# A recurrent attention with a three-way max feed-forward: the first up projection folded into the down projection, the weights loaded at other places

## The chip, the cores and the metric

The kernel runs on one core of a Trainium2 chip. The metric is the time of one execution on the device in microseconds (us), and less is better. Beside the runs there is one profiled execution, and the length of its trace, from the first to the last instruction, is called its span.

## The reference

A gated linear recurrence (4 batches, 8 heads, 768 steps, 48 values a head) gives 3072 rows of 384 values. They go through a feed-forward layer of three up projections, their maximum, and one down projection.

```python
state = alpha[:, :, t, :, None] * state + np.einsum('bhd,bhe->bhde', k[:, :, t], v[:, :, t])
y[:, :, t] = np.einsum('bhd,bhde->bhe', q[:, :, t], state)
...
h = np.maximum(np.maximum(x @ w1, x @ w2), x @ w3)
return (h @ w_out).astype(np.float32)
```

`w1`, `w2` and `w3` are 384 x 768 and `w_out` is 768 x 384, all of them float32, 1152 KB each. q, k, v and alpha are 4.7 MB each, and the output is 4.7 MB.

## The kernel before

**Tiles.** The sequence is cut into 6 chunks of 128 steps. With 4 batches this makes 24 units `u`, one chunk of one batch with its 8 heads. Two units make a group `n`, so there are 12 groups. The attention of a unit runs through `prep(u)` and `output(u)`: the logarithm of alpha on ACT (`decay`, L370), a running sum on PE (L413), two exponentials on ACT (L416, L418), products with q and k (L425, on POOL or DVE as the table `EARLY` says, else on POOL), a cast of v (L436, POOL, or L431, ACT), 8 transposes on PE (L446) with a copy out on DVE (L450), 8 score matmuls (L458), a masked copy on DVE (L464), the output matmuls (L481, L484), a scaled copy on ACT (L492), 3 transposes (L499) and a copy on DVE into `xT` (L503). `state(u)` carries the state to the next chunk (L517, L523 on DVE, L530 on POOL).

**The feed-forward layer of a group, `ffn(n)`.** For each of 3 pairs of 128 hidden columns and each of the 3 up projections, PE runs 6 matmuls with 256 moving columns (L554). The first projection is copied out of PSUM by ACT (L562); each of the other two goes through a maximum on DVE (L566). For each of the two units of the group there are then 6 matmuls with 384 columns for the down projection (L579), a copy on ACT (L587) and a store (L590).

**Loads.** All loads of q, k, v and alpha and all stores are issued from the SP queue. Loads of a group go into one of 5 buffers per tensor. Group 0 is loaded in halves (one unit each), every other group whole, 384 KB a tensor. The four weights are issued from the POOL queue by `weights(g, gate)` (L359), which casts to float16 on the way. Each waits for the k product of a unit: `w1` for unit 2, `w2` and `w3` for unit 3, `w_out` for unit 5.

**The order of the work** is written out at build time. Every step gives its engine, an assumed cost, a rank and what it reads and writes (`plan.step`); `Plan.order` goes through the steps in assumed time, puts them in order on each engine, and gives each its PSUM banks (8 in all). `Transfers` is its model of the two DMA queues. On the chip each engine works through its list in that order and waits where the next step is not ready. The feed-forward steps of a group have a rank `LEAD` behind the attention steps of the same group.

Of the kernel before, what the change touches and what calls it, by code (L numbers as in the profile page):

```python
# [21 lines left out]
NBANKS = 8  # L22
# [1 line left out]
TURN_RANK, TURN_COST = 2.0, 0.1  # L24
SP_FIRST = 0.9
QUEUES = ("SP", "POOL")
DMA_IN, DMA_OUT, DMA_SLOW = 0.9, 0.9, 1.0
DMA_BOTH = {"SP": 0.3, "POOL": 0.7}


class Transfers:


    def __init__(self):
        self.now = 0.0
        self.jobs = {e: [] for e in QUEUES}

    def add(self, e, arrival, work, i):
        self.jobs[e].append([arrival, work * DMA_SLOW, i])

    def next(self, commit=False):
        now = self.now
        left = {e: [list(j) for j in js[:1]] for e, js in self.jobs.items()}
        while True:
            heads = [(e, js[0]) for e, js in left.items() if js]
            if not heads:
                return None
            on = [(e, j) for e, j in heads if j[0] <= now + 1e-9]
            later = [j[0] for _, j in heads if j[0] > now + 1e-9]
            if not on:  # L50
                now = min(later)
                continue
            rate = DMA_BOTH if len(on) > 1 else dict.fromkeys(QUEUES, 1.0)
            e, j = min(on, key=lambda x: x[1][1] / rate[x[0]])
            end = now + j[1] / rate[e]
            if later and min(later) < end:
                for f, k in on:
                    k[1] -= (min(later) - now) * rate[f]
                now = min(later)
                continue  # L60
            if commit:
                for f, k in on:
                    self.jobs[f][0][1] = k[1] - (end - now) * rate[f]
                for f, k in heads:
                    if (f, k) not in on:
                        self.jobs[f][0] = k
                self.jobs[e].pop(0)
                self.now = end
            return end, j[2]


class Plan:
# [55 lines left out]
    def order(self):  # L128
# [19 lines left out]
                pending[self.steps[i][0]].add(i)  # L148
        free = dict(dict.fromkeys(HOP, 0.0), SP=SP_FIRST)
        bank_free = {b: 0.0 for b in range(NBANKS)}  # L150
        place, seq, recent = {}, [], []
        dma, mode = Transfers(), 0

        def finish(i, done):
# [15 lines left out]
        while len(seq) < n:  # L170
# [12 lines left out]
                if pick is not None and (best is None or pick < best[0]):  # L183
                    best = (pick, e)
            landing = dma.next()
            if landing and (best is None or landing[0] + DMA_OUT <= best[0][0]):
                end, i = dma.next(commit=True)
                self.landed[i] = end + DMA_OUT
                finish(i, end + DMA_OUT)
                continue  # L190
            (t, _, i), e = best
            _, cost, _, _, _, banks, load, m = self.steps[i]
# [5 lines left out]
            if e == "PE":  # L198
                if m != mode:
                    mode = m  # L200
                    cost += TURN_COST
                recent = [(a, b) for a, b in recent if b > t - 4.0]
                if sum(b - max(a, t - 4.0) for a, b in recent) < 2.0:
                    cost *= 2
                recent.append((t, t + cost))
            free[e] = t + cost
            seq.append((t, i))
            if load:
                dma.add(e, t + cost + DMA_IN, load, i)
            else:  # L210
                finish(i, t + cost + HOP[e])
            if i in follows:
# [6 lines left out]
def kernel(  # L219
# [76 lines left out]
    Zs = [homes(B, [P, NP, 2 * D], FP16, f"Z{i}_") for i in range(2)]  # L296
    e12s = homes(4, [P, HG // 2, 2], FP32, "e")
    Gs = homes(3, [P, HG // 2], FP32, "G")
    wcat = sb.tile([P, NFT, 3, DF], FP16, name="wcat")
    wo16 = sb.tile([P, NJ, DM], FP16, name="wo16")  # L300
    zero = sb.tile([P, 2 * P], FP16, name="zero")
    nc.vector.memset(zero, 0.0)
    for t in las:
        nc.vector.memset(t[:, :, D:], 0.0)
    for t in qks:
# [2 lines left out]
        for t in zz:  # L308
            nc.vector.memset(t, 0.0)

    plan = Plan({x: range(NBANKS) for x in ("Lp", "hp", "tp", "A", "yp", "xp", "pp", "gp", "op", "fill")})
    place = {}

    psall = pspool.tile([P, NBANKS, 512], FP32, name="psum")
# [10 lines left out]
    def banks2(key, dtype):  # L325
# [1 line left out]
        return both if dtype == FP32 else both.bitcast(dtype)  # L327

    live = {}
    LEAD = 7.5  # L330
    WAFTER = {2: (0,), 3: (1, 2), 5: (3,)}
    FILL = 0
    EARLY = {0: ("DVE", "DVE", "POOL"), 1: ("POOL", "DVE", "POOL"),
             3: ("DVE", "POOL", "POOL"), 5: ("POOL", "DVE", "POOL"),
             6: ("DVE", "POOL", "POOL"), 7: ("DVE", "POOL", "ACT")}


    views = {n: x.rearrange("b h s d -> s (b h) d") for n, x in
# [14 lines left out]
                      load=1.8 * (hi - lo) / HG)  # L353

    def weights(g, gate):
        w, dst = ((moe_w1, moe_w2, moe_w3, moe_w_out)[g],
                  wo16 if g == 3 else wcat[:, :, g, :])
        plan.step("POOL", 0.78, -1.0,
                  lambda: nc.gpsimd.dma_start(dst, w.rearrange("(t p) f -> p t f", p=P)),  # L359
                  reads=[gate], writes=[("w", g)], line="weights", load=3.5)  # L360


    def decay(n):
# [8 lines left out]
                      reads=[("a", n % 5, h) for h in range(lo // H, hi // H)],  # L372
                      writes=[("la", n % 3, h) for h in range(lo // H, hi // H)])

        if n == 0:
            ln(0, H)
            ln(H, HG)
        else:
            ln(0, HG)
        key = ("hp", n)  # L380

        def totals():
# [156 lines left out]
    def ffn(n):  # L539
        cb, g0 = divmod(n, B // UB)  # L540
        xT, hT = xTs[n], hTs[n % 3]
        npieces = 3 * (NJ // 2) + UB
        rank = [2 * n + LEAD + 2.0 * i / npieces for i in range(npieces)]
        for j in range(NJ // 2):
            for g in range(3):
                r = rank[3 * j + g]
                gk = ("gp", n, j, g)

                def grow(j=j, g=g, gk=gk):
                    live[gk] = bank(gk, [P, 2, TG], FP32)  # L550
                    for jj in range(2):
                        c0 = (2 * j + jj) * P
                        for kt in range(NFT):
                            nc.tensor.matmul(live[gk][:, jj, :], wcat[:, kt, g, c0:c0 + P],  # L554
                                             xT[:, kt, :], start=(kt == 0), stop=(kt == NFT - 1))

                plan.step("PE", 0.656, r, grow, banks=[gk],
                          writes=[gk] + ([("room", n % 3, j)] if g == 0 else []),
                          reads=[("room", n % 3, j)] * (g > 0) + [("w", g), ("xT", n, 0), ("xT", n, 1)])
                h = hT[:, 2 * j:2 * j + 2, :]  # L560
                if g == 0:
                    plan.step("ACT", 0.59, r, lambda h=h, gk=gk: nc.scalar.copy(out=h, in_=live[gk]),  # L562
                              reads=[gk], writes=[("hT", n % 3, j)])
                else:
                    plan.step("DVE", 0.69, r,
                              lambda h=h, gk=gk: nc.vector.tensor_max(h, live[gk], h),  # L566
                              reads=[gk, ("hT", n % 3, j)], writes=[("hT", n % 3, j)])
        for i in range(UB):
            b = g0 * UB + i
            m = n * UB + i  # L570
            r = rank[3 * (NJ // 2) + i]
            ok = ("op", m)
            parts = [(0, NJ)] if n < NG - 1 else [(0, NJ - 2), (NJ - 2, NJ)]
            for lo, hi in parts:
                def shrink(i=i, ok=ok, lo=lo, hi=hi):
                    if lo == 0:
                        live[ok] = bank(ok, [P, DM], FP32)
                    for kt in range(lo, hi):
                        nc.tensor.matmul(live[ok], hT[:, kt, i * P:(i + 1) * P], wo16[:, kt, :],  # L579
                                         start=(kt == 0), stop=(kt == NJ - 1))  # L580

                plan.step("PE", 0.1627 * (hi - lo), r + (0.5 if lo else 0.0), shrink,
                          banks=[ok] if lo == 0 else [], writes=[ok, ("ob room", m % 4)],
                          reads=[(x, n % 3, j) for x in ("hT", "room")
                                 for j in range(lo // 2, hi // 2)]
                          + [("w", 3)])
            plan.step("ACT", 0.49, r, lambda m=m, ok=ok: nc.scalar.copy(out=obs[m % 4], in_=live[ok]),  # L587
                      reads=[ok], writes=[("ob", m % 4)])
            plan.step("SP", 0.4, -2.0,
# [2 lines left out]
                      reads=[("ob", m % 4), ("ob room", m % 4)], load=0.5)  # L592


    def fill(count):
        for i in range(count):
            def run(i=i):
                if i == 0:
                    live[("fill",)] = bank(("fill",), [P, 2 * P], FP32)
                nc.tensor.matmul(live[("fill",)], zero[:, :P], zero, start=True, stop=True)  # L600

            plan.step("PE", 0.11, 99.0, run, banks=[("fill",)] if i == 0 else [],
                      writes=[("fill",)] if i == 0 else [], reads=[("fill",)] if i else [])

    fill(FILL)
    load(0, 0, H, "aqk")
    load(0, H, HG, "a")
    load(0, 0, H, "v")
    load(0, H, HG, "qkv")
    for n in range(NG):  # L610
        if n:
            load(n, 0, HG)
        decay(n)
        for u in range(n * UB - B, (n + 1) * UB - B):
            if u >= 0:
                state(u)
        for u in range(n * UB, (n + 1) * UB):
            prep(u)
            if u in WAFTER:
                for g in WAFTER[u]:  # L620
                    weights(g, ("qk", u % 7, 1))
            output(u)
        if n >= 4:
            ffn(n - 4)
    for n in range(NG - 4, NG):
# [36 lines left out]
```

## Time and profile before

| | us |
|---|---|
| median of 3 runs | 167.75 |
| lowest and highest run | 165.92, 167.81 |
| span of the profiled execution | 164.9 |

| engine | busy us in the span | what most of it is |
|---|---|---|
| PE | 145.3 | up projections L554 81.7, down projection L579 26.2 |
| DVE | 118.5 | maxima L566 47.7, masked scores L464 28.8 |
| ACT | 77.4 | copies L562 21.1, exponentials L416 and L418 11.9 each |
| POOL | 72.5 | products with q and k L425 41.2, state L530 15.7, casts of v L436 13.3 |

In the table busy time is the union of an engine's instructions. Matmuls overlap in it: a row such as "x648, 278 ns" gives the length of one matmul from its start to its modelled end, while a new one starts about every 109 ns. What a stream of matmuls costs is therefore read from the chain of waits, which gives the time from the first start to the next piece, not from the mean of one.

### The profile page before, as it was taken

How to read it: one execution, taken by the hardware profiler on the slowest of the kernel's cores; microseconds unless marked ns; L12 is line 12 of the kernel's file. 1: busy time of each engine (PE TensorE's matmuls, PEld its weight loads, DVE VectorE, ACT ScalarE, POOL GpSimd, SP SyncE). 2: the span in 40 equal slices, each digit the busy share in tenths (PEclk: the TensorE clock that was granted, in tenths of full speed). 3: DMA queues.
4: the chain of work that ended last, by engine and by line, in shares of the span. 5: the costliest groups of instructions: out<-in, count | busy, mean ns of one | idle time of the engine just before them, and what ended most of it. 6: DMA issues, size and time to landing. Idle time of an engine off the chain costs nothing.

```text
span 164.9 us, 4286 instructions
## 1 busy us (share of the span) xinstructions
PE 145.3 (88%) x1720; PEld 117.6 (71%) x1720; DVE 118.5 (72%) x204; ACT 77.4 (47%) x159; POOL 72.5 (44%) x104
## 2 busy tenths in 40 slices
PE   0555857869999999999999999999999999999991
PEld 0332635648867888889877898876898787878770
DVE  7464590088998999998999989993679685526460
ACT  3527362500466866557445765473634414252312
POOL 0043970070042899799917888829408000000000
PEclk9999985799999999999999999999999999999998
DMA  6999999999999999999899999995300020211112
GB/s 126 219 223 218 212 184 198 212 194 192 204 227 177 224 189 218 170 222 234 197 233 200 231 186 228 195 287 191 104 0 4 17 82 8 88 41 58 48 48 95
DMA packets 104884, 26.32 MB, mean 160 GB/s; under 512 B 99745, under 2 KB 104865, under 8 KB 104865
## 3 DMA queue, kind: packets, MB, share of 16 engines
q1 hardware_dynamic: 102592, 23.60, 70.0%
q0 software_dynamic: 1984, 2.36, 8.5%
q8 instruction: 13, 0.21, 0.5%
q10 hardware_dynamic: 288, 0.10, 0.3%
q14 instruction: 7, 0.05, 0.1%
HBM read 23.69 MB, written 4.72 MB: 172 GB/s over the span
## 4 chain that ended last, share of the span: by engine, by line
PE 75%; SPq 10%; DMA 9%; DVE 3%; issue 1%; ACTq 0%; ACT 0%; DVEq 0%
PE psum L554 40%; PE psum L579 14%; SPq L347 10%; DMA kn<-in_k_dram 9%; PE psum L446 5%; PE psum L458 3%; PE psum L484 2%; PE psum L499 2%; PE psum L481 2%; PE psum L413 2%; PE psum L517 2%; PE psum L385 1%; DVE qk L425 1%; DVE LA L464 1%; DVE qkT L450 1%
## 5 line engine op out<-in xcount | busy, mean ns | idle before, releaser
L554 PE MATMUL psum<-xT,wcat 128*128 128x256 f16 x648 | 81.7, 278 | 1.7 <-DMA wcat<-in_moe_w_dram 1.5
L554 PEld LDWEIGHTS <-wcat 128*128 128x128 f16 x648 | 62.3, 100 | 11.6 <-DMA wcat<-in_moe_w_dram 1.7
L566 DVE TENSOR_TENSOR hT<-psum,hT 128x512 f16<-128x512 f32 x72 | 47.7, 684 | 15.3 <-PE psum L554 13.0
L464 DVE TENSOR_TENSOR LA<-psum,c 128x1024 f16<-128x1024 f32 x24 | 28.8, 1217 | 6.5 <-PE psum L458 6.3
L425 POOL TENSOR_TENSOR qk<-kn,en 128x384 f16<-128x384 f32 x21 | 21.3, 1020 | 21.5 <-ACT en L418 11.5
L562 ACT CAST hT<-psum 128x512 f16<-128x512 f32 x36 | 21.1, 587 | 20.3 <-PE psum L554 19.5
L579 PE MATMUL psum<-wo,hT 128*128 128x384 f16 x144 | 26.2, 326 | 0.0
L425 POOL TENSOR_TENSOR qk<-qn,ep 128x384 f16<-128x384 f32 x20 | 19.9, 998 | 8.7 <-ACT ep L416 4.0
L587 ACT COPY ob<-psum 128x384 f32<-128x384 f32 x24 | 11.4, 481 | 22.4 <-PE psum L579 19.0
L492 ACT ACTIVATE xb<-psum,c 128x384 f16<-128x384 f32 x24 | 13.9, 585 | 14.9 <-PE psum L484 14.9
L436 POOL TENSOR_SCALAR v<-vn,c 128x384 f16<-128x384 f32 x23 | 13.3, 586 | 15.6 <-DMA vn<-in_v_dram 11.9
L530 POOL TENSOR_TENSOR Z<-U,G 48x192 f16<-48x192 f32 x32 | 15.7, 503 | 9.6 <-DVE U L523 8.5
L450 DVE COPY qkT<-psum 128x1024 f16<-128x1024 f16 x24 | 16.3, 685 | 4.7 <-PE psum L446 4.5
L446 PE MATMUL psum<-c,qk 128*128 128x128 f16 x192 | 16.1, 234 | 3.4 <-DVE qk L425 3.4
L579 PEld LDWEIGHTS <-hT 128*128 128x128 f16 x144 | 13.5, 98 | 7.6 <-DVE hT L566 0.2
L416 ACT ACTIVATE ep<-psum 128x384 f32<-128x384 f32 x24 | 11.9, 497 | 12.6 <-PE psum L413 12.0
L446 PEld LDWEIGHTS <-qk 128*128 128x128 f16 x192 | 13.1, 105 | 6.1 <-DVE qk L425 5.4
L370 ACT ACTIVATE la<-an 128x768 f16<-128x768 f32 (+1 forms) x13 | 10.3, 794 | 11.1 <-DMA an<-in_alpha_dram 11.1
L484 PE MATMUL psum<-v,LA 128*128 128x48 f16 x192 | 11.4, 186 | 2.9 <-DVE LA L464 2.9
L413 PE MATMUL psum<-la,c 128*128 128x384 f16 x24 | 8.5, 355 | 6.1 <-ACT la L370 6.1
L484 PEld LDWEIGHTS <-LA 128*128 128x128 f16 x192 | 9.7, 98 | 4.3 <-DVE LA L464 3.7
L418 ACT ACTIVATE en<-psum 128x384 f32<-128x384 f32 x24 | 11.9, 498 | 0.0
(30 smaller groups left out, 108.6 us busy)
## 6 DMA issues: line engine op xcount, KB each, us to landing
out_dram<-ob SPq DMA_DIRECT2D x24, 192.0 KB, 2.0
an<-in_alpha_dram SPq DMA_DIRECT2D x11, 384.0 KB, 5.8
qn<-in_q_dram SPq DMA_DIRECT2D x11, 384.0 KB, 6.0
kn<-in_k_dram SPq DMA_DIRECT2D x11, 384.0 KB, 5.6
vn<-in_v_dram SPq DMA_DIRECT2D x11, 384.0 KB, 5.7
wcat<-in_moe_w_dram POOLq DMA_DIRECT2D x3, 576.0 KB, 9.9
wo<-in_moe_w_out_dram POOLq DMA_DIRECT2D x1, 576.0 KB, 8.3
an<-in_alpha_dram SPq DMA_DIRECT2D x2, 192.0 KB, 3.4
```

Source lines behind the costliest of these rows:

```text
L347: nc.sync.dma_start(t[:, lo:hi], views[x][cb * P:(cb + 1) * P, g * HG + lo:g * HG + hi])
L425: nc.gpsimd if eng == "POOL" else nc.vector).tensor_mul(
L446: nc.tensor.transpose(live[tk][:, w, j, :], qk[:, w, 2 * j:2 * j + 2, :], ident)
L450: plan.step("DVE", 0.69, u, lambda: nc.vector.tensor_copy(out=qkT, in_=live[tk]), reads=[tk], writes=[("qkT", u % 3)])
L464: lambda: nc.vector.tensor_mul(LA.rearrange("p a b t -> p (a b) t"), live[Ak].rearrange("p a (b t) -> p (a b) t", t=P), maskA.unsqueeze(1) ...
L484: nc.tensor.matmul(yp[:, 2 * j + p, :], LA[:, p, j, :], v16[:, 2 * j + p, :], start=(cb == 0), stop=True, skip_group_check=True)
L492: lambda: nc.scalar.activation(out=xb, in_=live[yk].rearrange("p a b -> p (a b)"), func=AFT.Copy, scale=ysc),
L530: eng.tensor_mul(Zn[rows, :, cols], U[rows, :, cols], G[rows, i * NP:(i + 1) * NP].unsqueeze(2).broadcast_to([D, NP, D]))
L554: nc.tensor.matmul(live[gk][:, jj, :], wcat[:, kt, g, c0:c0 + P], xT[:, kt, :], start=(kt == 0), stop=(kt == NFT - 1))
L562: plan.step("ACT", 0.59, r, lambda h=h, gk=gk: nc.scalar.copy(out=h, in_=live[gk]), reads=[gk], writes=[("hT", n % 3, j)])
L566: lambda h=h, gk=gk: nc.vector.tensor_max(h, live[gk], h),
L579: nc.tensor.matmul(live[ok], hT[:, kt, i * P:(i + 1) * P], wo16[:, kt, :], start=(kt == 0), stop=(kt == NJ - 1))
```

## The change

With a = x w1, b = x w2 and c = x w3 the kernel now uses max(a, b, c) = a + relu(max(b - a, c - a)). It makes `wd`, the differences w2 - w1 and w3 - w1, and `w1o`, the product w1 w_out, once. The feed-forward layer of a group then has two up projections with the columns of `wd`, a relu on ACT for the first, one maximum on DVE for the second, and a down projection of 9 matmuls: 3 with `xT` and `w1o`, 6 with `hT` and `wo16`.

- `w1` and `w_out` are still cast loads from the POOL queue, now behind the k products of units 1 and 2. `w2` and `w3` are plain float32 loads from the SP queue, each in two parts (256 and 512 columns), placed among the loads of groups 0 and 1 by the table `FIRST`. Groups 0, 1 and 3 are loaded in halves.
- `subs` makes `wd` with four subtractions, three on DVE and one on POOL.
- `turned` transposes `w1` on PE (18 transposes) and copies it out on ACT (3 copies); `folded` makes `w1o` with 18 matmuls and 3 copies on ACT.
- `EARLY` moves some products between DVE, POOL and ACT: in all 5 of them stand on DVE in place of 7.
- `LEAD` goes from 7.5 to 8.5, and the planner's assumed costs of transfers and of the PE clock change. With them the order on each engine changes.

The list of SP now begins so (h and h' are the halves of a group, p0 and p1 the parts of a weight): a0h, q0h, k0h, a0h', k1h, k0h', q0h', w2p0, v1h, a1h, q1h, w2p1, v0h', v0h, q1h', a1h', w3p0, k1h', v1h', w3p1, then group 2 whole, group 3 in halves, group 4 whole. On POOL, `w1` is issued as the fourth step (behind both products and a cast of v), `w_out` as the seventh. On PE the 8 transposes of unit 2 and its scores come before the transposes of `w1`, then the outputs of units 0 to 2 and the product; then the first 12 matmuls of the up projection of group 0, the transposes of unit 3, and the next 24.

```diff
-    LEAD = 7.5
-    WAFTER = {2: (0,), 3: (1, 2), 5: (3,)}
+LEAD = 8.5
+EARLY = {0: ("DVE", "DVE", "POOL"), 3: ("DVE", "POOL", "POOL"), 4: ("POOL", "POOL", "POOL"),
+         5: ("POOL", "DVE", "ACT"), 7: ("DVE", "POOL", "POOL")}
+WEIGHTS = ((0, 1, "k"), (3, 2, "k"))
+WCUTS = (0, 256, 768)
+SUBS = {(1, 0): "DVE", (1, 1): "DVE", (2, 0): "POOL", (2, 1): "DVE"}
+FIRST = (("aqk", 0, 0, 1), ("a", 0, 1, 2), ("k", 1, 0, 1), ("kq", 0, 1, 2), ("w", 1, 0),
+         ("v", 1, 0, 1), ("a", 1, 0, 1), ("q", 1, 0, 1), ("w", 1, 1), ("v", 0, 1, 2),
+         ("v", 0, 0, 1), ("q", 1, 1, 2), ("a", 1, 1, 2), ("w", 2, 0), ("k", 1, 1, 2),
+         ("v", 1, 1, 2), ("w", 2, 1), ("aqkv", 2, 0, 2), ("k", 3, 0, 1), ("q", 3, 0, 1),
+         ("a", 3, 0, 1), ("v", 3, 0, 1), ("a", 3, 1, 2), ("kq", 3, 1, 2), ("v", 3, 1, 2))
...
     def weights(g, gate):
-        w, dst = ((moe_w1, moe_w2, moe_w3, moe_w_out)[g],
-                  wo16 if g == 3 else wcat[:, :, g, :])
+        w, dst = (moe_w_out, wo16) if g == 3 else (moe_w1, w1h)
...
+    def wload(g, part):
+        cols = slice(WCUTS[part], WCUTS[part + 1])
+        w = (None, moe_w2, moe_w3)[g]
+        plan.step("SP", 0.5, -1.0,
+                  lambda: nc.sync.dma_start(
+                      wst[g][:, :, cols], w.rearrange("(t p) f -> p t f", p=P)[:, :, cols]),
+                  writes=[("ws", g, part)], line="loads",
+                  load=3.2 * (cols.stop - cols.start) / DF)
+
+    def subs(g, part):
+        cols = slice(WCUTS[part], WCUTS[part + 1])
+        n, eng = NFT * (cols.stop - cols.start), SUBS[g, part]
+        plan.step(eng, 0.2 + n * (0.0023 if eng == "POOL" else 0.00106), 0.0 if g == 1 else 3.0,
+                  lambda: (nc.gpsimd if eng == "POOL" else nc.vector).tensor_sub(
+                      wd[:, :, g - 1, cols], wst[g][:, :, cols], w1h[:, :, cols]),
+                  reads=[("ws", g, part), ("w", 0)], writes=[("wd", g, part)])
+
+    def turned():
+        for i in range(NJ // 2):
...
+                        nc.tensor.transpose(live[key][:, jj, kt * P:(kt + 1) * P],
+                                            w1h[:, kt, c0:c0 + P], ident)
...
+    def folded():
+        for kt in range(NFT):
...
+                    nc.tensor.matmul(live[key], w1T[:, j, kt * P:(kt + 1) * P], wo16[:, j, :],
+                                     start=(j == 0), stop=(j == NJ - 1))
...
-            for g in range(3):
-                r = rank[3 * j + g]
+            for g in range(2):
+                r = rank[2 * j + g]
...
-                            nc.tensor.matmul(live[gk][:, jj, :], wcat[:, kt, g, c0:c0 + P],
+                            nc.tensor.matmul(live[gk][:, jj, :], wd[:, kt, g, c0:c0 + P],
...
-                    plan.step("ACT", 0.59, r, lambda h=h, gk=gk: nc.scalar.copy(out=h, in_=live[gk]),
+                    plan.step("ACT", 0.59, r,
+                              lambda h=h, gk=gk: nc.scalar.activation(out=h, in_=live[gk],
+                                                                      func=AFT.Relu),
...
-                        nc.tensor.matmul(live[ok], hT[:, kt, i * P:(i + 1) * P], wo16[:, kt, :],
-                                         start=(kt == 0), stop=(kt == NJ - 1))
+                        a, w = ((xT[:, kt], w1o[:, kt]) if kt < NFT
+                                else (hT[:, kt - NFT], wo16[:, kt - NFT]))
+                        nc.tensor.matmul(live[ok], a[:, i * P:(i + 1) * P], w,
+                                         start=(kt == 0), stop=(kt == nk - 1))
```

## The prediction

> **What bounds the kernel now.** I began with the page: busy shares, slices, the chain by engine (busy us by engine, PE in 40 slices, the chain by engine).
>
> ```profile
> PE 145.3 (88%) x1720; PEld 117.6 (71%) x1720; DVE 118.5 (72%) x204; ACT 77.4 (47%) x159; POOL 72.5 (44%) x104
> ...
> PE   0555857869999999999999999999999999999991
> ...
> PE 75%; SPq 10%; DMA 9%; DVE 3%; issue 1%; ACTq 0%; ACT 0%; DVEq 0%
> ```
>
> PE is full from the ninth slice to the end. The chain of waits in order of time (start, us, what) gives the place where that begins, and the pieces at the end:
>
> ```profile
> 17.39 15.66 DMA kn<-in_k_dram
> 33.14 1.39 DVE qk L425
> 34.58 0.84 PE psum L446 x12
> ...
> 145.56 1.95 PE psum L579 x12
> 147.51 5.89 PE psum L554 x54
> 153.41 1.95 PE psum L579 x12
> ...
> 159.29 1.64 PE psum L579 x10
> 161.00 0.28 ACT ob L587
> ```
>
> So 54 up matmuls with 256 columns cost 5.89 us, 0.109 each, and 12 down matmuls with 384 columns 1.95, 0.1625 each. PE ends at 161.2; the last copy and store make it 164.9, a tail of 3.7. Busy time by stages (PE, PEld, DVE, ACT, POOL, then clock, DMA share, GB/s):
>
> ```profile
> 20.00:30.00 10.00, 7.24 (x69) 5.11 (x70) 4.59 (x9) 4.70 (x11) 3.56 (x5) 0.70 1.14 190
> 34.58:161.24 126.66, 126.29 (x1534) 104.02 (x1534) 101.44 (x163) 61.41 (x128) 60.13 (x86) 1.00 0.73 151
> ```
>
> From 34.58 to 161.24 PE is busy 126.29 of 126.66 us at full clock. Two stretches then: a start that waits for transfers, at half rate, and 126.7 us in which only PE's work counts.
>
> **PE's work.** Removed: 216 of the 648 up matmuls, 216 x 0.109 = 23.6 us. Added in the down projection: 24 units x 3 matmuls x 0.1625 = 11.7. Added once: 18 transposes at 0.056 (8 of L446 take 0.45 late in the chain) = 1.0, and 18 matmuls x 0.1625 = 2.9. Net 23.6 - 15.6 = 8.0 us less.
>
> **DVE, ACT, POOL.** DVE loses 36 maxima of 0.684 (24.6 us), one memset and two products of 0.55, and gains three subtractions of 768, 1536 and 1536 values: from 0.545 at 384 (L523) and 0.684 at 512 (L566) the slope is 1.09 ns, so 0.96 + 1.80 + 1.80 = 4.6. It falls to about 97. ACT gains 3 copies of 768 (0.82 by L587 and L562) and 3 of 0.48, 3.9 us, and relu in place of a cast: no row shows relu, the 512 cast takes 0.587, an activation of 384 takes 0.497 and the one with a scale from a tile 0.585, so from about -0.1 to +0.1 for each of 36; I take 0. POOL gains a subtraction of 768 (twice the 1.0 of L425, 2.0) and two products of 1.0, and loses two issues of 0.8. ACT ends at 81, POOL at 75. PE still has the most; these edits cost nothing while it covers them. In the list of PE's waits after 34.6 nothing exceeds 0.2 us but the 2.2 at 34.58 itself.
>
> **The start.** This is what I must build. SP moves half loads at 0.94 us each (a0 lands at 3.93, the eighth half at 10.52); on POOL, w1 issued at 17.95 lands at 25.5, then w2 and w3 3.3 and 3.45 later, so a weight takes 3.3 us, some 4.3 after its issue. While POOL's three weights ran, SP's k of group 2, 1.8 us of transfer, took 15.66 from issue: the 16 engines' time is shared out, POOL's first.
>
> ```profile
> 17.95 2.50 POOL L359 DMA_DIRECT2D wcat<-in_moe_w_dram  x3
> 19.19 8.66 SPq L347 DMA_DIRECT2D vn<-in_v_dram  x1
> 25.57 6.61 PE L554 MATMUL psum<-xT,wcat 128*128 128x256 f16 x36 [1.51 <-DMA wcat<-in_moe_w_dram]
> 33.12 0.99 POOL L425 TENSOR_TENSOR qk<-kn,en 128x384 f16<-128x384 f32 x1 [9.24 <-DMA kn<-in_k_dram]
> 33.14 1.38 DVE L425 TENSOR_TENSOR qk<-kn,en 128x384 f16<-128x384 f32 x1 [8.25 <-DMA kn<-in_k_dram]
> ```
>
> After: no row shows float32 weights on SP. Bounds: 3.3 us each as the cast loads, or 5.4 at the rate of the 384 KB loads (1.8 us). Their rows of 1 and 2 KB are nearer to the weights of before than to the 192-byte rows of q, so 3.3. POOL's two products of unit 1 end near 11.4 (q0h' lands at 9.4), w1 is issued at 12.1, w_out at 16; they hold the transfers from 16.4 to 23.0. SP has landed all through w2p1 by 15.7 (3.93 + 9 x 0.94 + 3.3); then it waits behind them. Queued there are both v0 halves (24.9), q1h', a1h', w3p0 (28), k1h', v1h', w3p1. By sum, w3p1 lands at 3.93 + 15 x 0.94 + 4 x 3.3 = 31.2, or 32.1 with that gap. The subtraction that needs it ends at 33.9. PE's list stands at unit 1's output until v0 is cast, 24.9; then outputs, 18 transposes, three copies of w1 on ACT (to 28.6), 6 product matmuls at half rate (2.0), sums of group 1 and 12 more product matmuls: 33.4. There the up projection of group 0 begins; its second pair, which needs w3p1, comes 2.4 us later, past 33.9.
>
> New waits in this stretch: POOL's subtraction waits for w3p0 and ends at 30.1; behind it stand the k product of unit 3 and a cast, 1.6 us, whose reader, the transposes of unit 3, comes on PE at 34.7. DVE's first two subtractions wait for w1 (19.7) and end at 22.5, before the outputs whose copies stand behind them; the third waits until 32.1, and behind it stands the copy of unit 3's transposes, due after 35. All three are hidden as long as PE reaches its places no earlier than this.
>
> All later loads stand behind the same bytes as before, group 4's about 1 us later, so the load side does not move.
>
> By 33.4 PE has done: units 0 to 2 of attention 4.6, transposes and product 3.9, 8.5 us of full-rate work. Before, at 34.58, it had done 36 up matmuls (3.9), 36 L446 (2.0), 32 L458 (1.3), 6 L413 (1.0), 32 L484 (1.0) and 1.5 of small ones: 10.7. At 34.58 the changed kernel would stand at 9.7, 1.0 behind.
>
> **Sum.** -8.0 + 1.0 = -7.0 us, tail and small stalls kept: a span of 157.9 against 164.9. The span is 2.85 under the median of 167.75; I carry the difference over: 160.8 us. The one execution may belong to the lowest run (165.92), so the base is good to 2 us. With the full clock at once and w3 at 30, PE could start 2.5 earlier: 158.3.
>
> A rule on the first stretch: the 36 up matmuls at 25.57 took 6.61 us, 0.184 each, at a granted clock of 0.70. The Trainium skill (TensorE: Matmul & The Clock Gate, "What's actually happening") says the clock stays at half until a window of about 3.4 us has been busy, and the window runs freely; by it the new idle from 20 to 25 us could hold the half rate through the product and the first up matmuls. The trace agrees in kind; its price is worked out next, from rows.
>
> **Rivals.**
> Cold start: PE is still at half rate until the product and the first 12 up matmuls are through: 12 x 0.1625 + 12 x 0.109 = 3.3 us more, 164.1. For it: the half rate at 25 us. Against: from 25 on PE has few gaps.
>
> Blocked subtractions: DVE's product at 33.14 took 1.38 in place of 0.55 beside POOL's; it started to work when POOL's ended. The three DVE subtractions also read two SBUF tiles. The one on w3p1 may wait for up to 3.0 (POOL's subtraction and a product), and with 1.9 us of slack PE stands 1.1: 161.9. The Trainium skill (SBUF — State Buffer, "Who interferes with whom") states this: a DVE instruction with two SBUF inputs and a POOL instruction that reads SBUF exclude each other; the trace agrees by those 0.83 us.
>
> Attention paces: loads or POOL (9.85 of 10 us busy in 70 to 80) hold the attention back and PE idles where its work was taken. Then only the feed-forward after the loads' end near 110 gets cheaper: 270 up matmuls there are 5 groups x (1.96 - 0.98) = 4.9: 162.9. Against: DMA share falls to nothing after 115, and 11 groups of feed-forward can fill.
>
> Full gain: DVE at 97 in place of 118, no short stalls, an early start: 157 to 158.3.
>
> Late weights, slower: w2 and w3 at 5.4 each (+4.2) and POOL's two weights at 15.1 / 3 = 5.0 each (+3.4) while SP starves. All PE work waits behind w3p1 at 39.7: start at 41.0, +7.6, 168.4. It decides once w3p1 lands after about 39.5 (33.4 + 7.0 of start eats the gain); it needs 43 for 2%. Against: bytes are the same as before, and before, all four weights and all but one load of four groups had landed by 43.6.
>
> That PE is not relieved at all would need fewer matmuls taken than the list shows: 432 for 648 stand in it, so no chance.
>
> **How the numbers follow.** Forecast 0.53 (158.5 to 163.5), full gain 0.12, cold start 0.12, blocked subtractions 0.06, attention paces 0.09, late weights 0.08. The range 156.8 to 165.2 leaves out late weights, and the ends of the others. 2% of 167.75 is 3.4 us, about what a measurement here tells from no change: faster means under 164.4. That holds the forecast, the full gain, blocked subtractions and most of the paced case, and half of the cold start: 0.83. Same: the rest of those and most of late weights, 0.13. Slower: 0.04.
>
> **What would show it.** PE busy near 137; 432 up and 216 down matmuls; the saturated stretch beginning at 33 to 34 and lasting near 121 us; DVE near 97. The forecast is wrong if PE shows gaps of over a microsecond after 40 us, if w3p1 lands after 36, or if the transposes and product run on at half rate past 34.

## The result and the profile after

| | before, us | after, us |
|---|---|---|
| median (4 runs each) | 167.78 | 162.30 |
| lowest and highest run | 165.92, 167.96 | 161.44, 163.05 |
| span of the profiled execution | 164.9 | 161.3 |

The ratio is 0.9705, with a 95% interval from 0.9644 to 0.9766. A second measurement on another chip gave 162.64 us and 0.9728 [0.9684, 0.9771]. So the gain is 3%, 5.5 us by the medians, where the prediction's sum had 7.0. Runs more than 1.5% above the fastest of their kernel (two in experiment 1, one each in 4, 6 and 7) count in the medians below but not in the ratios.

The two spans differ by only 3.6 us, and both ends of that need a word. In every run with both on record, the time is the span and 1.73 to 1.84 us (163.05 beside 161.3). By that the profiled execution of before stands for about 166.7, 1.1 under its median, and the one of after is the slowest of its four, 0.75 above its median: 3.6 + 1.1 + 0.75 = 5.5.

The page of after, the same three lines as before (busy us by engine, PE in 40 slices, the chain that ended last by engine):

```profile
PE 136.2 (84%) x1612; PEld 104.6 (65%) x1612; DVE 99.6 (62%) x168; ACT 80.9 (50%) x167; POOL 77.0 (48%) x105
...
PE   0534387978897999899969799999999999999990
...
PE 40%; SPq 26%; DMA 20%; POOL 4%; ACT 3%; issue 3%; DVE 1%; ACTq 0%; POOLq 0%
```

The busy times came out within 3 us of what was worked out (137, 97, 81 and 75 for PE, DVE, ACT and POOL). But PE is no longer full from the ninth slice on: it shows 7s, 8s and a 6 up to the 23rd slice (4 us each, so up to 93 us). In the chain PE's share fell from 75% to 40%, and SP's queue and transfers took its place; up to 43.9 us it now runs through SP's queue alone. Busy times by stage, from 34 to 118 us (PE, PEld, DVE, ACT, POOL, then clock, DMA share, GB/s), first of before, then of after:

```profile
34.00:118.00 84.00, 83.05 (x1105) 68.61 (x1106) 75.00 (x122) 46.00 (x98) 56.81 (x81) 1.00 1.04 207
```

```profile
34.00:118.00 84.00, 78.73 (x1079) 61.82 (x1077) 66.47 (x112) 49.86 (x109) 62.95 (x88) 1.00 1.05 206
```

PE lost 5.3 of 84 us in after and 1.0 in before, at the same clock and the same DMA rate. The chain of after in order of time (start, us, what) says where:

```profile
68.10 4.78 DMA out_dram<-ob
76.41 5.00 DMA an<-in_alpha_dram
81.43 0.85 ACT la L454
...
82.94 6.98 DMA an<-in_alpha_dram
89.95 0.85 ACT la L454
```

Twice in this stretch the end was set by a load of alpha, its logarithm on ACT, and PE behind them; ahead of that stands a store of the output. (A third such load stands in the chain at 43.94, and two loads of v from 92.00 to 104.35.) PE's list of waits over 36 to 118 us (us in all, times, longest) has the same reading:

```profile
PE psum L495 <- ACT la L454: 4.4, 5, 1.4
PE psum L528 <- POOL qk L507: 0.5, 1, 0.5
```

L495 is the running sum of attention. While PE stood at it, the rows of six groups were ready for the feed-forward and 4.5 groups of up projections had been done (at 80.7 us; at 89.5 us seven and 5.3). So there was work for PE that its list did not offer. That is the question of the experiments: why not.

### The profile page after: what moved, and what is told of

Same layout as the page of the kernel before. It is cut to its first block, busy times and chain, and to the rows that moved or that the text cites. A ratio compares the mean times of both kernels' runs of the same rounds, so it can differ in the third digit from the quotient of the medians.

```text
span 161.3 us, 4047 instructions
## 1 busy us (share of the span) xinstructions
PE 136.2 (84%) x1612; PEld 104.6 (65%) x1612; DVE 99.6 (62%) x168; ACT 80.9 (50%) x167; POOL 77.0 (48%) x105
## 4 chain that ended last, share of the span: by engine, by line
PE 40%; SPq 26%; DMA 20%; POOL 4%; ACT 3%; issue 3%; DVE 1%; ACTq 0%; POOLq 0%
SPq L377 22%; PE psum L669 16%; PE psum L638 15%; DMA an<-in_alpha_dram 11%; DMA vn<-in_v_dram 6%; SPq L399 4%; DMA out_dram<-ob 3%; PE psum L528 3%; ACT la L454 2%; POOL Z L612 2%; PE psum L495 1%; POOL v L518 1%; PE psum L540 1%; POOL qk L507 1%; PE psum L581 1%
## 5 line engine op out<-in xcount | busy, mean ns | idle before, releaser
L638 PE MATMUL psum<-xT,wd 128*128 128x256 f16 x432 | 54.2, 273 | 0.9 <-DVE wd L408 0.9
L638 PEld LDWEIGHTS <-wd 128*128 128x128 f16 x432 | 40.4, 98 | 7.6 <-DVE wd L408 1.2
L653 DVE TENSOR_TENSOR hT<-psum,hT 128x512 f16<-128x512 f32 x36 | 24.3, 685 | 16.2 <-PE psum L638 15.7
L507 POOL TENSOR_TENSOR qk<-qn,ep 128x384 f16<-128x384 f32 x21 | 21.0, 998 | 19.7 <-DMA qn<-in_q_dram 9.2
L648 ACT ACTIVATE hT<-psum 128x512 f16<-128x512 f32 x36 | 21.1, 597 | 15.8 <-PE psum L638 15.4
L669 PE MATMUL psum<-wo,hT 128*128 128x384 f16 x144 | 27.3, 326 | 0.0
L507 POOL TENSOR_TENSOR qk<-kn,en 128x384 f16<-128x384 f32 x22 | 22.6, 1028 | 0.9 <-PE psum L566 0.4
L518 POOL TENSOR_SCALAR v<-vn,c 128x384 f16<-128x384 f32 x23 | 15.5, 676 | 15.7 <-DMA vn<-in_v_dram 15.5
L669 PEld LDWEIGHTS <-hT 128*128 128x128 f16 x144 | 14.1, 98 | 9.3
L495 PE MATMUL psum<-la,c 128*128 128x384 f16 x24 | 8.3, 345 | 9.9 <-ACT la L454 9.9
L669 PE MATMUL psum<-w1o,xT 128*128 128x384 f16 x72 | 15.6, 326 | 0.0
L585 DVE COPY xT<-psum 128x384 f16<-128x384 f16 x24 | 8.4, 353 | 10.9 <-PE psum L581 8.4
```

The lines of the kernel that those rows point to most:

```text
L507: nc.gpsimd if eng == "POOL" else nc.vector).tensor_mul(
L518: lambda: nc.gpsimd.tensor_scalar(out=v16, in0=ld["v"][n % 5][:, hs], scalar1=vsc, scalar2=1.0, op0=AOP.mult, op1=AOP.mult),
L638: nc.tensor.matmul(live[gk][:, jj, :], wd[:, kt, g, c0:c0 + P], xT[:, kt, :], start=(kt == 0), stop=(kt == NFT - 1))
L648: lambda h=h, gk=gk: nc.scalar.activation(out=h, in_=live[gk], func=AFT.Relu),
L669: nc.tensor.matmul(live[ok], a[:, i * P:(i + 1) * P], w, start=(kt == 0), stop=(kt == nk - 1))
```

## The experiments

Three theories. **A**: the plan made at build time takes a load of a group for 1.8 us; at 206 GB/s its 384 KB take 1.9. By comparing the landings with the times that the kernel's own plan gives them, a load is late by 1.7 us at 31 us, 3.8 at 50, 5.8 at 81 and 8 at 104; attention steps therefore stand too early in PE's list. **B**: loads or POOL pace the attention, whatever the list (the rival "attention paces"). **C**: the feed-forward is stopped. SP's list is written out with the first store behind the loads of many groups; the output has four tiles (`ob`) and the hidden rows three sets (`hT`), so down projections stop after two groups, up projections after five, and PE's list has little but attention left.

For C the output tile in after (its copy on ACT and its store on SP's queue; min/median/max ns, first and last start):

```profile
L677 ACT COPY ob<-psum x24: 459/478/485, 37.0 to 157.5; 128x384 f32<-128x384 f32 x24
L680 SPq DMA_DIRECT2D out_dram<-ob x24: 332/333/3047, 68.1 to 158.1; - x24
```

A first tile full at 37.5 us is stored at 68.1. The first four copies start at 37.05, 40.17, 57.10 and 58.34; the fifth at 73.72, right after that store landed (68.10 + 4.78 = 72.88). Before had the same late store:

```profile
L587 ACT COPY ob<-psum x24: 468/479/523, 46.2 to 161.4; 128x384 f32<-128x384 f32 x24
L590 SPq DMA_DIRECT2D out_dram<-ob x24: 332/332/3110, 74.7 to 161.9; - x24
```

What it could hide behind it was larger: two groups' down and five groups' up projections are 2 x 1.95 + 5 x 5.89 = 33.4 us of PE work by the prediction's rows, and in after 2 x 2.92 + 5 x 3.93 = 25.5 (18 L669 take 2.92, 36 L638 3.93 at the end of its chain). This is an estimate of the stock, not a measurement.

**1. The plan's load at 1.95.**

```diff
-                      load=1.8 * (hi - lo) / HG)
+                      load=1.95 * (hi - lo) / HG)
```

> The changed kernel, with one number of the planner changed: a load of 384 KB is assumed to take 1.95 us instead of 1.8. Theory A (the plan puts running sums ahead of feed-forward that is ready, because it believes the loads come earlier than they do; in the trace after, PE waits 4.4 us for logarithms of alpha after 30 us): these waits fall under 1.5 us, PE ends 3 to 5 us earlier, 157 to 159.5 us. Theory B (the loads themselves pace the attention and PE has nothing else to do then): 161 to 163 us, the idle time of PE between 40 and 110 us stays at about 8 us.

Measured 164.91 (162.70 to 165.90), ratio 0.9818 [0.9738, 0.9899]: no gain over the change, and above both expectations. The profile is of the run of 165.90. The waits on alpha are gone, and PE is busy 29.62 and 29.77 us in the windows of 30 us that lose 2.0 and 2.6 in after. New losses came behind them (windows of the profiled run; PE busy, clock, DMA share, GB/s):

```profile
40.00:70.00 30.00, 29.62 (x421) 1.00 1.10 206
70.00:100.00 30.00, 29.77 (x422) 1.00 1.06 216
100.00:118.00 18.00, 15.46 (x179) 0.81 0.86 183
```

From 104 to 111 us seven groups of up projections were done and nine to ten ready; PE did attention in short pieces and waited between them, and the clock fell. Eight units of down projections, four groups, were done too, so the three hidden sets were full. The ninth unit stood behind the fifth store, whose tile was full at 78.2 us. It went out, first of four, at 108.16:

```profile
108.16 2.94 SPq L680 DMA_DIRECT2D out_dram<-ob  x4
```

So A has the right place for the first stall and does not explain the time. This is what led to C.

**2. The same line in before.**

> The kernel before with the same number 1.95. Theory A: PE had hardly a wait after 34.6 us, so there is little to take away: 165.5 to 168 us, and the difference from the changed kernel with 1.95 becomes 7 to 10 us. Theory B: the same time as before and the difference stays near 5.5 us.

167.14, ratio 1.0041 [1.0016, 1.0065]: the time lies where both put it, as before has no such stall to lose. The difference from the changed kernel with 1.95 became 2.2 us, which neither expected.

**3. Eight output tiles and 1.95.**

```diff
-    obs = homes(4, [P, DM], FP32, "ob")
+    obs = homes(8, [P, DM], FP32, "ob")
...
-            plan.step("ACT", 0.49, r, lambda m=m, ok=ok: nc.scalar.copy(out=obs[m % 4], in_=live[ok]),
-                      reads=[ok], writes=[("ob", m % 4)])
+            plan.step("ACT", 0.49, r, lambda m=m, ok=ok: nc.scalar.copy(out=obs[m % 8], in_=live[ok]),
+                      reads=[ok], writes=[("ob", m % 8)])
```

> The changed kernel with the planner's load at 1.95 us and 8 output tiles (ob) instead of 4. Theory C (the first store is issued at 68 us behind the loads in SP's list, although its tile is full at 37; with 4 output tiles the down projections stop until a store has landed, with them the 3 hidden tiles and the up projections, so PE has only the attention left and waits for its loads): PE's waits after 40 us fall from about 8 to under 3 us, and 157.5 to 160.5 us. Theory B (the loads pace everything until 113 us): 161 to 164 us.

159.14 (158.81 to 160.99), ratio 0.9537 [0.9479, 0.9596]. The window from 34 to 118 us, columns as above:

```profile
34.00:118.00 84.00, 83.07 (x1133) 66.02 (x1134) 70.91 (x116) 53.07 (x113) 61.99 (x87) 1.00 1.03 214
```

PE's one wait left in 36 to 118 us is 0.4 on an `xT`. The store still starts at 71.7; with eight tiles nothing waits for it. C's range held. B is out as the main cause: with the same loads and the same POOL the attention did not hold PE up.

**4. Eight output tiles alone.**

> The changed kernel with 8 output tiles alone, the planner's load left at 1.8 us. Theory C with the plan at fault too: the list still puts running sums of alpha where the loads have not landed, so part of the waits stay: 159.5 to 162.5 us. If the tiles alone are at fault: 157.5 to 159.5. Theory B: 161 to 164.

165.35, ratio 0.9874 [0.9841, 0.9907], outside all three expectations and slower than the change itself. PE's busy time in the window is 78.36, as in after; the waits have only moved:

```profile
PE psum L528 <- POOL qk L507: 4.1, 6, 1.4
PE psum L495 <- ACT la L454: 0.9, 2, 0.6
```

A list made for loads that land too early is wrong for eight tiles as well as for four. Why it comes out slower than the change, and not the same, is not settled.

**5. Both edits in before.**

> The kernel before with both edits (8 output tiles, load planned at 1.95 us). Theory C: PE was full from 34.6 us on, so there is nothing to fill: 165.5 to 168 us. If the two edits are worth something by themselves: under 164.5 us.

165.15, ratio 0.9875 [0.9854, 0.9897]: 2 us are gained here too, between the two expectations. In the profiles they come mostly from the start: PE was busy 27.3 of the first 40 us, against 24.45 in before's, and 77.8 of the next 78, against 77.6. Busy time at half rate is less work; counted in matmuls at their full-rate price, PE stood 1.3 us further at 40 us, of 1.6 between the two spans. So the edits are not worth 3 us to the change and nothing to before. With both edits on either side, on one chip, the change is worth 165.15 - 159.14 = 6.0 us.

**6. No fold product.** The transposes of `w1` and the product are left out and `w1o` is zero, so the output lacks x w1 w_out.

```diff
+    nc.vector.memset(w1o, 0.0)
...
-        if g == 0:
-            turned()
-        else:
-            folded()
```

> The changed kernel without the transposes of w1, their copies, the product w1 w_out and its copies; w1o is zero, so the output lacks x w1 w_out. It leaves out 36 PE instructions, 3.9 us at full rate. If PE's work sets the end, as in the sum of the prediction: 158 to 159.5 us. If the first up projections wait for the last part of w3 (landing 31.3, its subtraction done at 33.1 us) and the product stands in that wait: 161 to 163 us.

164.21 (162.36 to 165.68), ratio 0.9781 [0.9718, 0.9843], for 3.9 us less of PE work: nothing gained, and above both expectations. PE had next to nothing to do from 21 to 25 us (its longest wait there, 2.99 us, was for a cast of v on POOL), and the first up projections ran at half rate (start, us, engine, line, what, and in brackets the wait ahead):

```profile
27.67 4.05 PE L635 MATMUL psum<-xT,wd 128*128 128x256 f16 x18
31.51 1.06 PE L525 MATMUL psum<-c,qk 128*128 128x128 f16 x8
```

From start to start that is 3.84 us for 18, 0.213 for one, where the full rate is 0.109; it lasted until 32.6 us. (The clock column shows 1.00 for this stretch, so the half rate is read from the starts.) The one-time product costs nothing here: it fills a gap in which PE would wait for the attention's inputs.

**7. The stores issued earlier, four tiles, and 1.95.** In the plan a load of q, k, v or alpha may now be issued only when the load four places ahead has landed, so that stores take earlier places in SP's list: the first three have 27, 30 and 41 steps ahead of them, where the change has 45, 49 and 56. The chip runs the same steps with the same tiles.

```diff
+    sent = []
+
+    def ahead(key):
+        sent.append(key)
+        return [sent[-1 - 4]] if len(sent) > 4 else []
...
-            plan.step("SP", 0.5, -1.0, run, line="loads",
+            plan.step("SP", 0.5, -1.0, run, line="loads", reads=ahead((x, n % 5, lo // H)),
```

> The changed kernel with 4 output tiles as it has them, the planner's load at 1.95 us, and one rule more in the plan: a load is not issued before the landing of the load four places ahead of it, so that stores stand in SP's list where they fall in time. Theory C (stores behind loads hold the output tiles): the first store is issued before 55 us instead of at 68, the waits after 40 us stay under 3.5 us, 158 to 161 us, as with 8 output tiles. If the count of tiles and not the place of the stores is what counts: 161.5 to 165 us.

157.94 (157.22 to 159.63), ratio 0.9425 [0.9374, 0.9476], just below C's range and the fastest version of this study. Its output tile, and then its window from 34 to 118 us:

```profile
L683 ACT COPY ob<-psum x24: 459/478/485, 37.2 to 151.7; 128x384 f32<-128x384 f32 x24
L686 SPq DMA_DIRECT2D out_dram<-ob x24: 332/556/2966, 38.4 to 152.3; - x24
```

```profile
34.00:118.00 84.00, 83.52 (x1137) 66.71 (x1134) 69.99 (x115) 53.01 (x115) 63.52 (x89) 1.00 1.06 213
```

The first store starts 30 us earlier, and four tiles are enough. Beside experiment 1 the rule on the loads is the only edit (the order of other steps moves with it). So this and experiment 3 show C from two sides: more room, or room given back sooner, each with the load at 1.95.

The plan's own end of PE, worked out from each kernel's `Plan`, tells the same before any run: 150.4 us for the change, 157.7 with 1.95 (experiment 1), 151.7 with eight tiles besides (3) and 151.8 here. On the chip PE ended at 157.4, 160.3, 153.2 and 151.6. With truer load times the plan itself thus asks 6 us for four tiles with late stores; with 1.8 it did not see them (150.9 with eight tiles, experiment 4).

**8 to 11. The fold and the places by themselves.** `fold_alone` folds with before's places, queues, `EARLY`, `LEAD` and assumed costs (all four weights as cast loads on POOL). `places_alone` keeps three projections with the places of after; `w2` and `w3` come as float32 on SP and DVE and POOL cast them. Both were also run with eight tiles and 1.95.

Parts of the edits against the changed kernel, first of the one and then of the other:

```diff
-WEIGHTS = ((0, 1, "k"), (3, 2, "k"))
+WEIGHTS = ((0, 2, "k"), (1, 3, "k"), (2, 3, "k"), (3, 5, "k"))
-LEAD = 8.5
+LEAD = 7.5
```

```diff
-                      wd[:, :, g - 1, cols], wst[g][:, :, cols], w1h[:, :, cols]),
+                      out=wcat[:, :, g, cols], in_=wst[g][:, :, cols]),
```

> The fold alone: all four weights as cast loads from POOL behind the gates of the kernel before, the loads in its order, its table of early products, its LEAD and its assumed costs of transfers and clock; the two differences, the product and the changed feed-forward as in the changed kernel. If the 8.0 us of matmul work are the gain and the new places give nothing of it: 160 to 163 us. If the new places of the weights are needed for it (w1o must wait for w_out, which lands at 42 us in the kernel before, and the down projections wait with it): 163.5 to 167 us.

> The new places alone: three up projections and three-way maximum as in the kernel before, but w2 and w3 loaded as float32 on SP in the places of the changed kernel and cast by DVE and POOL, with its table of early products, LEAD and assumed costs. Matmul work is that of the kernel before, so with PE as the bound nothing but the start can move: 165 to 168 us. If the places make the gain: 162 to 164 us.

> The fold alone with 8 output tiles and the load planned at 1.95 us. Its loss between 40 and 110 us was only 2.8 us, so theory C gives it at most 2 us: 161.5 to 163.5 us; its long wait at 28 us (6.7 us for the k load of group 2 behind the three weights) stays. With the new places on top (159.1) the places are then worth 2.5 to 4.5 us.

> The new places alone (three up projections, no fold), with 8 output tiles and the load planned at 1.95 us. It ran at 175.6 without these edits, where PE lost 5.7 us between 40 and 110 us and 3 us more than before at the start. If theory C holds there too: the middle loss falls under 2.5 us, 170 to 172.5 us; the start's loss stays. If the places cost it all by the start and the clock: 174 to 176 us.

Ratios to before on the same chip:

| | places of before | places of after |
|---|---|---|
| three projections | 1 | 1.0547 [1.0497, 1.0597], 175.59 us |
| folded | 0.9856 [0.9796, 0.9915], 163.92 us | 0.9705, 162.30 us |
| three projections, both edits | 0.9875, 165.15 us | 1.0217 [1.0172, 1.0261], 170.96 us |
| folded, both edits | 0.9674 [0.9625, 0.9724], 161.99 us | 0.9537, 159.14 us |

`places_alone` missed its expectations, which lay between 162 and 168. The places cost 9 us without the fold (5.7 by the ratios with both edits) and gain 2.3 to 2.5 with it; they are not a gain of their own. Of the 9 us, 3.2 are lost until 40 us and 5.9 after, counted as in the balance below. `fold_alone` fell in its second range, though its longest wait is not the one for `w_out` that is named there, and with both edits the two kernels fell in the ranges that C gave. What holds `fold_alone` up is the start that before has (a piece of PE's timeline, the wait in brackets):

```profile
34.73 1.46 PE L529 MATMUL psum<-c,qk 128*128 128x128 f16 x12 [6.44 <-DVE qk L508]
```

The load of k behind three cast weights, 15.66 us in before, is there again with 15.97. The new places remove that wait. Why three projections lose so much by the same places was not taken apart.

## Why the prediction was right, and where it was not

The balance of PE, from the starts of its matmuls. "Work" is every matmul at its full-rate price, "lost" the rest of the time up to PE's end: waits and half rate.

| us | before | after | difference | forecast |
|---|---|---|---|---|
| PE's work | 134.7 | 126.8 | -7.9 | -8.0 |
| lost until 40 us | 24.1 | 22.3 | -1.8 | +1.0 |
| lost from 40 us to PE's end | 2.3 | 8.2 | +5.9 | 0 |
| PE's end | 161.2 | 157.4 | -3.8 | -7.0 |

**PE's work** was right to 0.1 us, with 432 up and 216 down matmuls. That the price of 0.109 and 0.1625 us, taken from the chain, holds for the changed kernel is what made it so.

**"Tail and small stalls kept"** is the step that failed, in its second half. The tail was kept (3.7 before, 3.8 after). The stalls were not: 5.9 us more. PE's removed work had been the cover of a store that came 30 us late, and of loads that land behind the plan. The prediction named the place in its rival "attention paces" ("PE idles where its work was taken") and argued it down with "11 groups of feed-forward can fill". They did not. The list had attention in these places, made for loads that land up to 8 us earlier, and with four output and three hidden tiles no more than five groups may be under way until the first store is done. With truer loads in the plan the tiles did run out, later (experiment 1: seven groups of up and four of down projections from 104 to 111 us). The prediction's own sign of being wrong, gaps of over a microsecond after 40 us, is there twice: 1.38 us at 82.33 and 1.15 at 90.84. The late store could have been read in the profile of before, where the first copy into `ob` starts at 46.2 and the first store at 74.7. Experiments 3 and 7 took the stalls away, and the spans became 157.0 and 155.4, where the sum had 157.9 with none added. Part of that is not the stalls: before itself gains 2 us by the edits, and the change measured on equal terms is worth 6.0 us.

**The start** was off by 2.8 us on the good side, and by luck this hid half of the failure. Of its landings the last was right: w3p1 at 31.29 (computed 31.2 to 32.1). Those in the middle were not: it had SP stand behind POOL's two weights from 16.4 to 23.0 and v0 land at 24.9, but the halves of v0 landed at 17.49 and 21.14, `w1` at 20.91 (19.7) and `w_out` at 25.33 (23.0). The subtraction and the second pair of up projections followed as said (PE's timeline of after):

```profile
27.07 2.11 PE L437 MATMUL psum<-wo,w1T 128*128 128x384 f16 x12
29.02 1.47 PE L638 MATMUL psum<-xT,wd 128*128 128x256 f16 x12
...
33.12 1.48 PE L638 MATMUL psum<-xT,wd 128*128 128x256 f16 x12 [0.88 <-DVE wd L408]
```

What was mis-sized is PE's work ahead of the first up projection: from v0's cast at 24.9 to 33.4 by the prediction, and from 23.9 to 29.0 in the trace. (That the cast came near 24.9 is luck: the load was 3.8 us earlier, and the cast itself took 2.1 us longer than others, as told below.) The 18 transposes and the outputs of two units ran from 20.96 to 24, as soon as `w1` landed, not behind that cast; the copies of `w1T` ended at 24.95 (computed 28.6); and the product ran at the full rate (its last 12 matmuls took 1.95 us, 0.1625 each; from 23.7 on transposes start every 56 ns, before that every 107) where six of its matmuls had been put at half. So PE had 24 up matmuls and the transposes of unit 3 behind it when it came to wait 0.9 us for w3p1.

**Cold start** (164.1): the idle of 20 to 25 us did not hold the clock down in after, but it does where the product is taken away (experiment 6). The rival's mechanism is real here, and the transposes and the product prevent it.

**Blocked subtractions** (161.9): the one on w3p1 was not blocked, as POOL's had ended at 29.2. The same lock fell on a q product instead (engine, line, operation, then the wait ahead; first POOL, then DVE):

```profile
27.54 1.64 POOL L408 TENSOR_TENSOR wd<-ws,w1h 128x768 f16<-128x768 f32 x1 [3.61 <-DMA ws<-in_moe_w_dram]
...
27.85 1.75 DVE L507 TENSOR_TENSOR qk<-qn,ep 128x384 f16<-128x384 f32 x1 [0.71 <-ACT ep L498]
```

DVE's product took 1.75 in place of 0.55 and ended 0.4 us behind POOL's subtraction. The Trainium skill (SBUF — State Buffer, "Who interferes with whom") has this as an exclusive lock on the ports that DVE and POOL share; the trace agrees by those 1.2 us. PE did not wait for it.

The prediction had DVE's first two subtractions end at 22.5, ahead of what stands behind them on DVE. They ended at 23.56, and POOL's cast of v0 beside them took 2.71 us in place of 0.58:

```profile
20.93 2.63 DVE L408 TENSOR_TENSOR wd<-ws,w1h 128x768 f16<-128x768 f32 x2 [1.11 <-DMA w1h<-in_moe_w_dram]
...
21.23 2.71 POOL L518 TENSOR_SCALAR v<-vn,c 128x384 f16<-128x384 f32 x1 [3.06 <-DMA vn<-in_v_dram]
```

The cast ended 0.4 us behind them, as DVE's product did behind POOL's subtraction, so it is read as the same lock. PE's output of that unit came at 23.98, right behind the cast; the product behind it then waited for `w_out` (25.33), so this too cost little.

**Late weights** (168.4) did not come: the last weight on SP landed where 3.3 us for each put it. **Full gain** (157 to 158.3) is reached by experiment 7 (157.94), not by the change. That POOL, DVE and ACT stay hidden was right: the relu took 597 ns and the cast 587.

**The carried 2.85 us** between span and median is 1.75 that every run has and 1.1 by which the profiled execution of before was below its median. Between the traces, which the sum describes, the miss is 3.4 us (161.3 against 157.9), between the medians 1.5: the two profiled executions lie on opposite sides of their medians, by 1.1 and 0.75. That the number came so near is luck in this part too.

**What stays open**: why a load takes 1.95 us by its landings and not 1.8 (between 45 and 110 us most of after's loads land 1.2 to 2.2 us behind the transfer ahead, and eight 2.4 to 3.1); why eight tiles alone are slower than the change; why `places_alone` loses its start. The loads' place was changed only through the plan's cost and the rule of experiment 7; other orders of loads and stores were not tried.

## What to carry to other kernels

When work is taken from the engine that bounds a kernel, ask what that work had covered: list the buffers between the stages, count how many groups can be under way until the first of them is given back, and compare that stock with the waits of the loads. In a list that is written out ahead, a store that is placed behind loads in one queue is a lock on its tile. More tiles paid here only together with truer transfer times in the plan; the earlier place was tried only with them. A one-time computation in a gap of PE may cost nothing, and here it kept the clock up.

## What was not expected of the hardware

The clock can fall in the middle of a run without a long wait. In experiment 1 PE was busy 2.46 of 3.50 us and then 2.21 of 3.40, in many short pieces with no wait over 0.73 us, and from 109.4 to 116.2 us its matmuls took twice their time:

```profile
102.50:106.00 3.50, 2.46 (x43) 1.00 1.33 226
106.00:109.40 3.40, 2.21 (x45) 1.00 0.90 173
```

That the clock fell is seen in this one profile: 6.8 us at half of 164.1 make the mean of 0.979 that this run has. All four runs of that kernel have a mean granted clock of 0.974 to 0.989, and those of the change 0.995 to 1.000 in both measurements; but runs of before lie between 0.975 and 1.000, so a mean does not tell where a clock was lost. The Trainium skill (TensorE: Matmul & The Clock Gate, "What's actually happening") has the half rate after an idle window of about 3.4 us: the length of the slow stretch, 6.8 us, agrees with two such windows, but no window before it was idle. The price, as an estimate, is half of the 6.5 us that PE was busy in this stretch, about 3.3, and it comes on top of the waits themselves.
